# Halo rows of two head pairs copied by DMA from SyncE, a summing matrix zeroed by GpSimd, and a new order of work in a sparse-attention and hardswish kernel

## The chip, the cores and the metric

One core of a Trainium2 chip. The metric is device time of one execution, in microseconds (us). The engines go by the profile's names: PE (TensorE), DVE (VectorE), ACT (ScalarE), POOL (GpSimd), SP (SyncE). Each works through its own list of instructions in order; between engines, semaphores hold an instruction back until what it needs is done.

## The reference

```python
B, H, S, D = 4, 8, 768, 64          # q, k, v
block, window = 32, 16
k_sum = k.reshape(B, H, 24, 32, D).max(axis=3)
v_sum = v.reshape(B, H, 24, 32, D).mean(axis=3)
scores_l = q @ k.T / 8              # masked to |i - j| < 16
scores_s = q @ k_sum.T / 8 + log(32)
a = softmax(concat([scores_l, scores_s]))
x = a @ concat([v, v_sum])          # to [3072, 512]: tokens, heads * D
h = x @ w_in                        # [3072, 2048]
out = (h * clip(h + 3, 0, 6) / 6) @ w_out
```

Each query looks at its neighbours within 16 positions, and at 24 block summaries of the whole sequence. What comes out of all heads goes through two large matrix products with a hardswish between them.

## The kernel before

**Tiles.** Queries go in 12 blocks of 64. For each block the keys and values that it can see are 96 rows: the block itself and 16 on each side. So `vaug[i]` (i is the batch modulo 2) has, for every head and query block, 120 rows on partitions: rows 0 to 31 are the halo, rows 32 to 95 come straight from memory (L424), and rows 96 to 119 are the block means of v. The halo of block t is a copy of rows 64 to 95 of block t - 1, so it can be made out of what is on the chip already. `halo(c, x)` makes it for batch 0, for head pair c (heads 2c and 2c + 1) and half x: x = 0 are blocks 6 to 11, which are worked on first, x = 1 are blocks 0 to 5, the first blocks' half, with block 0 taken from block 11 in a second copy. In the kernel before each is done by DVE or ACT through `copy` (L479). For the other batches the halo is loaded from memory.

**Block sums.** `vsum_first(g)` forms the means of v for pairs 2g and 2g + 1 of batch 0: 24 products (L620) of `ind[:, t]`, a 96 x 32 matrix that says which row belongs to which block, with rows 0 to 95 of `vaug`. Rows 0 to 31 of `ind` must be zero, since halo rows would be counted twice. `ind` is made by POOL (L341 to L344), and its first 32 rows are zeroed by DVE (L347). The sums are copied to `vf` and from there spread over `vaug` rows 96 to 119, for x = 0 early, for x = 1 later.

**Attention.** `k_step` and `q_step` transpose k and q of batch 0 on PE; `scores` forms products of keys and queries (L588), ACT takes exponentials (L597), DVE masks them (L601); `values` multiplies with `vaug` (L709, and L711 with L713 where the means of pairs 2 and 3 come from `vf`). `finish` takes reciprocals (L743), scales (L747), and transposes the result on PE (L781) into `xt`, the input of the MoE half.

**MoE half.** `f1(s, ft)` forms one 128-column piece of h for 384 tokens (L800: four products of 384 columns; for the first three pieces of the first 384 tokens, three groups of four with 128 columns). ACT forms r (L805), DVE the gate (L807). `f2` multiplies with w_out (L820), 16 products for each 128 tokens. Eight stages s of 384 tokens, 512 columns.

**Order.** The kernel records its operations in a plan. `ORDER` is a string with every operation's name in the order in which they are to be planned. A name is a tag and a number: `h031.1` is the second operation of `halo(3, 1)`, `u01.0` the sums of pairs 2 and 3, `v02.0` the first value products of query blocks 4 and 5 in order of work, `K`, `Q`, `V`, `I`, `O` are loads, `F` and `G` the two MoE products. A letter behind a colon chooses the engine where there is a choice (A: ACT, D: DVE, P: POOL, S: SP). `Plan.run` goes through the string, gives each operation a begin from a table of costs, and the operations are then emitted in order of begin. The framework below adds the waits: an instruction waits for the writers, emitted before it, of any rows that it reads, and for the readers of rows that it overwrites.

**Products without use.** Where the plan leaves PE idle within the first 22 us of planned time, `keep` puts products on a constant tile, `idle` (L910), 128 x 512, into a free bank.

**Loads.** All loads are issued by POOL and land by one set of 16 DMA engines. SP issues nothing before the first output is stored at 62.27 us.

Of the kernel before, what the change touches and what calls it, by code (L numbers as in the profile page):

```python
# [15 lines left out]
D = 64  # L16
BLK = 32
# [12 lines left out]
c.0 z1.0:A z3.1:A z0.1:A K00.0 z1.1:D e.3 z0.2 z2.0:D c.8 K01.0 c.1 K02.0 Q000.0 c.2 Q010.0 c.3 k00.0 z0.0:D e.1 z3.0:D c.4  # L30
k01.0 V00.0 V01.0 V02.0 V03.0 c.6 Q01w2.0 Q01w1.0 I0.0 Q01w0.0 k01.2:A k00.1 e.0 k01.1 z2.2 z3.2 z2.1:D k01.4 z1.2 k03.0
k00.3:A k00.2:A k01.3:A q010.0 q010.1:A q000.0 k02.0 q000.1:A k00.4 s000.0 q030.0 s010.0 q020.0 s000.1 s010.1 e.2 k03.1
k02.1 h000.0:D h001.0:D k03.4 c.7 q020.1:D k03.3:A q030.1:A k03.2:A s000.2 s010.2 Q11w0.0 I1.0 I2.0 u00.0 k02.4 h010.0:D
u00.2:A k02.2:A h021.0:D h020.0:D u00.1:D u00.3:D u00.5:D h030.0:D s030.0 s030.1 s020.0 s020.1 s030.2 u01.0 s020.2 I3.0 O0.0
O1.0 K13.0 O2.0 O3.0 K11.0 K10.0 K12.0 u01.2:A u01.1:A v00.0 v01.0 v02.0 v01.1 v00.2 v00.3 v02.2 v02.3 v01.2 v01.3 v00.1
v00.6 v02.1 v00.4 v00.5 v02.4 v02.5 k02.3:A v00.7:A u00.4:A v01.4 v00.8 v00.9:A v01.5:A v02.6 v02.7:A F00.0 F00.10 F00.1
q021.0 q001.0 F00.2 q021.1:A h011.0:D u00.6:D h031.0:D u01.3:D q001.1:D F00.3 F00.11 F00.12 q031.0 F00.4 F00.5 F00.6 F00.7
F00.15 q031.1:A F00.13 F00.8 F00.16 c.5 F00.14 F00.9 F00.17 u01.4:D s031.0 q011.0 s031.1 q011.1:A F01.6 F01.7 s031.2 F01.8
F01.3 F01.4 F01.0 F01.1 F01.5 c.9 F01.2 s001.0 s011.0 s011.1 s011.2 s001.1 s001.2 F02.0 F02.9 F02.1 F02.2 s021.0 F01.9
F02.10 F02.11 F03.0 F02.3 s021.1 F01.10 s021.2 F03.1 F01.11 v03.0 v04.0 F03.2 v03.1 v04.1 v04.2 v03.2 F03.6 F03.9 G02.0  # L40
v03.3 v05.0 F02.4 F03.10 F03.7 F02.5 F03.8 v05.1 v05.2 F02.6 v03.4:A F02.7 v04.3 F03.3 v04.4:D Q11w3.0 V13.0 V12.0 V10.0
V11.0 Q11w4.0 Q11w2.0 Q11w5.0 Q11w1.0 v05.3 G02.1 F03.11 F02.8 v05.4:A F03.4 F03.5 F10.0 F10.1 F10.6 F10.7 F10.2 F10.8 F11.0
F11.1 F11.3 F11.2 F11.4 F11.5 F13.0 F13.1 F13.2 F12.9 F12.6 F12.10 F12.11 F12.7 F12.8 F12.0 F13.6 F12.1 F13.7 F12.2 F13.8
F13.9 F10.3 F13.10 F10.4 F10.5 F13.11 w13.0 G02.2 F10.9 F11.9 F10.10 F10.11 G02.3 F11.6 F12.3 w10.0 w12.0 w11.0 w12.1:D
G02.4:A F12.4 F11.10 w11.1:A G01.0 G01.1 G01.2 G01.3 u1.0 F11.11 G01.4:A F12.5 w11.2 w13.1:A F11.7 w10.1:A u1.1:A u1.6:A
w10.2 w13.2 w10.3:A u1.4:D F11.8 w13.3:D w11.3:D G00.0 G00.1 G00.2 q100.0 q120.0 q110.0 q100.1:A s100.0 s100.3 s100.1 G00.3
q130.0 q120.1:D q110.1:D w12.2 w12.3:D s100.2 u1.8:D u1.2:D s100.4 q130.1:D K23.0 h11.0 K22.0 h10.0 K21.0 Q21.0 K20.0 Q20.0
Q23.0 Q22.0 V22.0 h21.0 V21.0 h20.0 V20.0 V23.0 G00.4:A s110.0 G00.5 F13.3 G12.0 s110.1 s110.3 s120.0 F13.4 s120.3 s120.1
G12.1 G12.2 F13.5 u1.3:D s120.2 s110.2 h1w.0:A s130.0 s130.1 s130.3 G12.3 G12.4:A G12.5 G01.5 s130.2 s110.4 v10.0 s130.4
v10.1 v10.2 v10.5 v10.6 G11.0 G11.1 v12.0 v10.3 u1.9:A u1.7:A u1.5:A v12.1 v12.2 s120.4 w20.0 w20.3 G11.2 v10.4:A v10.7  # L50
v10.8:A v12.3 v12.4:A G11.3 v15.0 v15.1 v15.2 F20.0 G11.4:A F20.1 F20.3 F20.4 F20.6 v13.0 F20.7 F20.2 F20.5 F20.8 v13.5
v13.1 v13.2 F20.9 F22.0 F21.0 w20.2:A F20.10 F22.1 v13.3 F21.1 F20.11 F22.2 F21.2 w20.1 v13.6 F21.6 F22.6 F21.3 v13.4:A
F21.7 F22.7 v15.3 G10.0 v13.7 F21.4 v15.4:A w20.5:A v13.8:A F21.8 F22.8 F21.5 F22.3 F21.9 w20.4:A F22.4 F21.10 F22.9 G10.1
s200.0 w22.0 w21.0 F22.10 w22.2:A s200.3 s200.1 F22.11 F22.5 w23.0 F21.11 G10.2 F23.6 G10.3 F23.0 F23.3 V30.0 V33.0 V31.0
h30.0 h31.0 V32.0 Q33.0 Q31.0 K33.0 Q32.0 K32.0 Q30.0 K31.0 K30.0 F23.7 w21.2:A w21.1 F23.8 G10.4:A F23.1 w21.5:A F23.4 u2.0
u2.1:A u2.2:A F23.9 w21.3 w21.4:D F23.5 w22.1 F23.2 G10.5 G02.5 F23.10 s210.0 F30.9 G20.0 s210.3 u2.4:A u2.5:D w23.1 F23.11
w22.3 G20.1 F30.0 F30.1 F30.10 s210.1 w22.5:A F30.2 w22.4:D F30.11 u2.3:D G20.2 F30.3 G20.3 F30.4 w23.5:A F30.5 w23.3 s210.2
F30.6 G20.4:A F30.7 s210.4 F30.8 s220.0 w23.2:A s220.3 s220.1 w23.4:A F31.3 F33.3 G22.0 u3.0 F31.4 u3.1:A F33.4 s220.4
s220.2 s200.2 F31.5 F32.6 F32.7 s200.4 F33.5 F32.8 s230.0 G22.1 F31.0 G22.2 h2w.0:A s230.1 s230.3 s230.2 s230.4 F32.3 v20.0
F31.9 F31.1 F31.2 v20.1 v20.4 v20.2 v20.5 u3.5:A F31.10 F31.11 F32.0 G22.3 v22.0 v25.0 v20.3 v22.1 v22.2 v22.3 v20.6 F31.6  # L60
u3.3:A G22.4:A F32.4 F31.7 F32.1 F31.8 F32.5 F32.2 w30.1 v22.5:P v22.7:P G21.0 G21.1 G21.2 F33.6 G21.3 F33.7 G11.5 G20.5:S
v22.6:S v22.4:S F33.8 F33.9 F33.0 F32.9 v25.1 w31.1 v25.2 G21.4:A F33.1 G21.5:P G22.5:S F32.10 F32.11 G32.0 G32.1 G32.2
F33.10 F33.11 F33.2 G32.3 h3w.0:A G32.4:A w30.0 w30.3 w31.5:A w30.2:A u3.4:A v23.0 w31.0 G30.0 G30.1 G30.2 F40.0 F42.9
w30.4:A v23.4 v23.5 v23.1 v23.2 v23.3 v25.3 F40.1 F42.10 F40.3 F40.4 F40.2 F42.11 F41.3 F40.5 v23.6 F40.6 F40.9 F41.4 F40.7
F40.10 F41.5 G30.3 G30.4:A F40.8 F40.11 w31.3 F43.9 w30.5:A F43.10 F41.9 F43.6 F41.10 F43.7 F43.11 F41.11 u3.2:A v25.4:S
v25.7:P v25.6:P G32.5:S v25.5:S G30.5:P G31.0 F41.0 F41.6 F43.8 w31.2:D w31.4:D w33.0 F42.6 F41.7 F41.1 F41.8 F42.7 w32.0
F41.2 F42.8 s310.0 G31.1 s310.3 s310.1 F42.3 G31.2 F43.3 F42.0 F42.4 w32.2:A F43.4 F42.1 F42.5 w32.3 F43.0 F43.1 F43.5 F42.2
F43.2 w32.1 w32.5:D s300.0 G31.3 s300.1 w32.4:A s300.3 G31.4:A F50.9 F50.0 F50.6 F50.1 s320.0 w33.1 w33.3 F50.2 G41.0 G41.1
G41.2 F51.9 F50.7 s320.1 s320.2 w33.4:D F50.8 s300.2 w33.5:A w33.2:A s320.3 F50.10 s330.0 s330.1 s330.3 F50.11 s320.4 s310.2
s330.2 G41.3 F51.0 F52.0 G41.4:A v30.0 F52.1 F51.1 s300.4 s330.4 s310.4 v30.4 v30.1 v30.5 F52.2 v30.2 F51.2 v30.3 v30.6  # L70
G42.0 G42.1 G42.2 G42.3 F51.6 v35.0 v32.0 G42.4:A F51.7 F51.10 F52.6 G40.0 G40.1 F52.7 G40.2 v32.1 v32.2 v32.3 v35.1 F51.11
F52.8 F51.8 F50.3 F52.3 F53.3 F50.4 F52.4 F53.4 v35.2 F50.5 G40.3 F51.3 G42.5:S v32.6:P v32.4:P G31.5:S v32.5:S v32.7:S
F52.5 F53.5 F53.6 F51.4 G40.4:A F53.7 G40.5:P F51.5 F53.0 v33.0 F52.9 G50.0 F52.10 F53.1 F53.8 v33.4 v33.5 v33.1 F52.11
F53.2 F53.9 G50.1 G50.2 F53.10 F53.11 G50.3 F60.0 F60.3 F60.1 F60.4 G50.4:D v33.2 F60.2 F60.5 v33.3 v33.6 G52.0 F63.3 F63.4
F63.5 v35.3 G52.1 F61.9 F62.0 F62.1 F61.10 G52.2 G52.3 F61.11 G52.4:D F63.9 F63.10 F62.2 F63.11 F62.9 G51.0 F62.10 F62.11
G50.5:P G41.5:P v35.4:P v35.7:S G52.5:S v35.6:S v35.5:S F61.0 F61.3 F61.4 F61.1 G51.1 F61.5 F61.6 F61.7 F61.8 F60.6 F60.7
F61.2 F60.8 G51.2 F60.9 F60.10 F60.11 F63.0 F63.1 F63.2 G51.3 G51.4:D G51.5:P F63.6 F62.3 F62.4 F62.5 F62.6 G62.0 G62.1
F62.7 F63.7 F62.8 F63.8 G62.2 G62.3 G62.4:A F70.0 F72.9 G60.0 F71.3 F70.1 F71.4 F70.2 F71.5 F72.10 F73.0 G60.1 F73.1 F72.11
F73.2 F70.9 F70.6 F70.7 F70.8 F72.0 G60.2 F72.1 F70.10 F70.11 F72.2 F73.6 F73.7 F73.8 G60.3 G60.4:A F71.9 F72.6 F72.7 F71.10
F71.11 F72.8 G61.0 F70.3 F70.4 F70.5 G61.1 F73.9 F73.10 F73.11 F71.0 F71.1 F71.6 F71.7 F71.8 F71.2 G61.2 F72.3 F72.4 G61.3  # L80
G70.0 G61.4:A F72.5 G62.5:P G61.5:S G71.1 G71.3 F73.3 F73.4 G70.1 G70.2 F73.5 G60.5:S G70.3 G72.0 G72.1 G70.4:D G70.5 G71.5
G72.2 G72.3 G71.0 G71.2 G72.4:A G72.5 G71.9 G71.10:D G71.11 G71.4 G71.6 G71.7:A G71.8
"""

BANKS = ("S", "h", "o")


SLOW = 4.5
TURN = 0.11
LATER = 19.0  # L90
KRAW = 1.6
LAT = {"SP": 0.1, "PE": 0.16, "ACT": 0.08, "DVE": 0.07, "POOL": 0.15}

# [126 lines left out]
def kernel(  # L220
# [83 lines left out]
    def const_ops():  # L304
# [35 lines left out]
        def blocks():  # L340
# [3 lines left out]
            nc.gpsimd.affine_select(out=ind[:], in_=ind[:], compare_op=ALU.is_ge, fill=0.0, base=2 * BLK - 1, channel_multiplier=-1,  # L344
                                    pattern=[[-QB, NQ], [BLK, 32]])
        op("POOL", 1.6, blocks, w=["ind"], prio=-78.5)
        op("DVE", 0.2, lambda: nc.vector.memset(ind[0:BLK], 0.0), w=["ind"], prio=-78)  # L347

        def edges(i):
            t = vaug[i]  # L350
# [606 lines left out]
```

## Time and profile before

| | us |
|---|---|
| time, three runs | 218.79, 220.41, 220.47 |
| median | 220.41 |
| the profiled execution, its own time | 218.78 |
| its span | 217.1 |

| engine | busy us | share of the span | instructions |
|---|---|---|---|
| PE | 207.0 | 95% | 2124 |
| DVE | 165.0 | 76% | 330 |
| ACT | 136.9 | 63% | 271 |
| POOL | 91.0 | 42% | 117 |

| stage (us) | PE busy | DVE busy | ACT busy | POOL busy | DMA share |
|---|---|---|---|---|---|
| 8 to 12 | 3.87 | 3.43 | 2.72 | 3.86 | 1.80 |
| 12 to 16 | 2.75 | 3.27 | 3.22 | 4.00 | 2.44 |
| 16 to 20 | 3.63 | 3.60 | 2.94 | 3.77 | 1.67 |
| 20 to 24 | 3.94 | 3.87 | 3.43 | 2.66 | 1.66 |
| 24 to 28 | 2.96 | 3.87 | 2.72 | 3.11 | 1.24 |
| 28 to 32 | 3.90 | 3.86 | 3.84 | 2.30 | 1.24 |
| 32 to 36 | 3.83 | 3.92 | 2.20 | 1.20 | 1.96 |

The stages are 4 us long, so 4.00 is an engine without a gap. A DMA share over 1 means that packets of more than one transfer were under way in each DMA engine. The span runs from the first to the last recorded event of the program; the time of the execution is 1.7 us longer. In a line of a timeline the first number is the start, the second how long the group of like instructions lasted, then follow engine, line of the kernel, operation, what it writes and reads, how many, and in brackets how long the engine had been idle and what ended that. Ends of products on PE are modelled, so neighbouring groups overlap by 0.1 to 0.2 us.

### The profile page before, as it was taken

To read this page: it belongs to the slowest core of one execution; us is meant where nothing else is said; L and a number is where in the kernel's file an instruction comes from. 1 tells how busy PE (TensorE), PEld (TensorE's weight loads), DVE (VectorE), ACT (ScalarE), POOL (GpSimd) and SP (SyncE) were. 2 spreads that over 40 slices of the span, in tenths; PEclk is the share of its full clock that TensorE was granted. 3 is DMA by queue.
4 is the path that set the end of the run, shared out by engine and by line. 5 is a ranking of instruction groups with operands and counts; after the bars stand their busy time and mean duration, and the time that the engine had idled before them with its cause. 6 is when DMAs were issued, how large, how long until landed. Compare 5 with 4: busy or idle time off the path is not lost.

```text
span 217.1 us, 5338 instructions
## 1 busy us (share of the span) xinstructions
PE 207.0 (95%) x2124; PEld 116.4 (54%) x2151; DVE 165.0 (76%) x330; ACT 136.9 (63%) x271; POOL 91.0 (42%) x117
## 2 busy tenths in 40 slices
PE   6979899999999999999999999999999999999994
PEld 2546656554554565555555555545555555555543
DVE  6889999779798899988898898987865756163310
ACT  8687795664789688998844788963342344345301
POOL 7997944254697856527254073000542401100000
PEclk9999999999999999999999999999999999999999
DMA  5999999999999999999936045000540452100212
GB/s 75 159 155 182 205 207 184 168 138 155 106 125 154 190 148 151 131 204 156 107 35 142 0 77 95 3 0 3 130 91 15 107 90 57 51 0 0 97 51 98
DMA packets 129705, 23.03 MB, mean 106 GB/s; under 512 B 120816, under 2 KB 127152, under 8 KB 129680
## 3 DMA queue, kind: packets, MB, share of 16 engines
q0 software_dynamic: 112656, 17.34, 119.2%
q1 hardware_dynamic: 17024, 5.34, 10.1%
q8 instruction: 17, 0.28, 0.5%
q14 instruction: 8, 0.07, 0.1%
HBM read 29.62 MB, written 6.29 MB: 165 GB/s over the span
## 4 chain that ended last, share of the span: by engine, by line
PE 84%; POOL 4%; DMA 4%; DVE 4%; issue 2%; ACT 2%; POOLq 0%
PE h L800 37%; PE o L820 32%; PE h L820 5%; DMA vaug<-in_v_dram 4%; PE S L709 3%; PE S L588 2%; DVE g L807 2%; POOL vaug L424 1%; PE S L641 1%; POOL first L383 1%; PE S L781 1%; DVE at L601 1%; ACT at L597 1%; POOL first L391 1%; ACT ot L479 0%
## 5 line engine op out<-in xcount | busy, mean ns | idle before, releaser
L800 PE MATMUL h<-x,win 128*128 128x384 bf16 (+1 forms) x536 | 94.3, 319 | 1.3 <-DVE g L807 1.3
L807 DVE SCALAR_TENSOR_TENSOR g<-r,h 128x384 bf16<-128x384 f32 x128 | 67.6, 547 | 29.8 <-ACT r L805 27.5
L805 ACT ACTIVATE r<-h 128x384 f32<-128x384 f32 x128 | 60.6, 492 | 45.9 <-PE h L800 44.4
L820 PE MATMUL o<-wout,g 128*128 128x512 bf16 x312 | 79.0, 379 | 1.6 <-issue 0.5
L800 PEld LDWEIGHTS <-win 128*128 128x128 bf16 x536 | 49.6, 98 | 36.5 <-issue 1.9
L820 PEld LDWEIGHTS <-g 128*128 128x128 bf16 x400 | 38.0, 98 | 36.7
L769 POOL DMA_DIRECT2D x<-y x28 | 17.2, 622 | 40.9 <-issue 22.0
L597 ACT ACTIVATE at<-S 120x768 bf16<-120x768 f32 x32 | 24.7, 813 | 2.4 <-PE S L588 2.4
L424 POOL DMA_DIRECT2D vaug<-in_v_dram x16 | 15.1, 945 | 13.0 <-issue 3.9
L479 ACT COPY ot<-o 128x512 f32<-128x512 f32 x18 | 10.6, 587 | 13.0 <-PE o L820 12.0
L601 DVE TENSOR_TENSOR at<-at,mask 96x768 bf16<-96x768 bf16 x28 | 14.5, 547 | 2.2 <-ACT at L597 1.8
L747 DVE TENSOR_TENSOR xn<-S,rc 128x512 bf16<-128x512 f32 (+1 forms) x24 | 15.7, 661 | 0.5
L413 POOL DMA_DIRECT2D kraw<-in_k_dram x8 | 10.7, 1339 | 8.2 <-issue 4.2
L479 ACT COPY vaug<-vs 24x1536 bf16<-24x1536 bf16 (+1 forms) x10 | 12.1, 1212 | 0.2
L678 DVE TENSOR_REDUCE red<-kaug 128x24 bf16<-128x768 bf16 x12 | 11.1, 941 | 0.1
L820 PE MATMUL h<-wout,g 128*128 128x256 bf16 (+1 forms) x63 | 10.7, 325 | 0.1
L832 POOL DMA_DIRECT2D out_dram<-ot x7 | 4.0, 567 | 14.0 <-DVE ot L479 8.5
L588 PEld LDWEIGHTS <-kaug 64*128 64x128 bf16 x384 | 6.8, 95 | 5.5 <-issue 3.3
L709 PEld LDWEIGHTS <-at 120*64 120x64 bf16 x360 | 6.8, 111 | 4.5 <-issue 3.7
L588 PE MATMUL S<-qT,kaug 64*128 64x64 bf16 x384 | 8.8, 191 | 0.2 <-ACT qT L479 0.2
L910 PE MATMUL o<-idle 128*128 128x512 bf16 x17 | 7.4, 572 | 1.6 <-DVE idle L306 1.5
L709 PE MATMUL S<-vaug,at 120*64 120x65 bf16 x352 | 8.2, 197 | 0.1
(107 smaller groups left out, 181.9 us busy)
## 6 DMA issues: line engine op xcount, KB each, us to landing
vaug<-in_v_dram POOLq DMA_DIRECT2D x22, 192.0 KB, 11.1
out_dram<-ot SPq DMA_DIRECT2D x14, 256.0 KB, 3.1
win<-in_moe_w_in_dram POOLq DMA_DIRECT2D x4, 512.0 KB, 8.5
wout<-in_moe_w_out_dram POOLq DMA_DIRECT2D x4, 512.0 KB, 14.5
kraw<-in_k_dram POOLq DMA_DIRECT2D x8, 192.0 KB, 13.8
out_dram<-ot POOLq DMA_DIRECT2D x5, 256.0 KB, 2.4
first<-in_k_dram POOLq DMA_DIRECT2D x6, 192.0 KB, 6.3
first<-in_q_dram POOLq DMA_DIRECT2D x6, 192.0 KB, 9.0
```

Of the source, the lines that this page charges most:

```text
L424: op("POOL", 0.95, lambda: nc.gpsimd.dma_start(out=o[BLK:WIN, lo:hi, 0:D], in_=rows[:, lo:hi]), w=[("v", b % 2, c)], prio=prio, dma=1.25, ...
L479: {"ACT": nc.scalar.copy, "DVE": nc.vector.tensor_copy, "POOL": nc.gpsimd.tensor_copy}[eng](o, i)
L588: nc.tensor.matmul(X[p, half].slot[:, j, i * QB:(i + 1) * QB], kaug[p][rows, t], qT[rows, p, t * QB:(t + 1) * QB], start=not masked, stop= ...
L597: op("ACT", act(2 * HALF), lambda a=a, x=x: nc.scalar.activation(a, x.slot[0:KEYS, :, 0:HALF], AF.Exp, scale=scl), r=[x], w=[("at", p, hal ...
L601: op("DVE", 0.57, lambda m=m, half=half: nc.vector.tensor_tensor(m, m, mask[:, low(half):low(half) + HQ].unsqueeze(1).to_broadcast([WIN, 2 ...
L709: nc.tensor.matmul(y, a[:, cols], vaug[b % 2][0:KEYS, h, t, 0:D + 1], start=True, stop=True)
L747: nc.vector.tensor_tensor(o, src[..., 0:D], r.unsqueeze(len(r.shape)).to_broadcast(list(o.shape)), op=ALU.mult)
L769: QUEUE[eng].dma_start(out=xt[s].slot[32 * a:32 * a + 32].rearrange("p k (t c j) -> p (k t) c j", t=3, c=4)[:, :, c], in_=ys[s].slot[32 * ...
L800: nc.tensor.matmul(h.slot[:, lo * 128:hi * 128], w_in_sb[:, kt, ft * 128:(ft + 1) * 128], xt[s].slot[:, kt, lo * 128:hi * 128], start=(kt ...
L805: op("ACT", act(HALF), lambda: nc.scalar.activation(r.slot[:], h.slot[:, 0:HALF], AF.Relu, bias=0.5, scale=1.0 / 6.0), r=[h], w=[r], prio= ...
L807: op("DVE", dve(HALF), lambda: nc.vector.scalar_tensor_tensor(gt[s].slot[:, ft], r.slot[:], 1.0, h.slot[:, 0:HALF], op0=ALU.min, op1=ALU.m ...
L820: nc.tensor.matmul(o.slot[:, a:z], gt[s].slot[:, ft, ts * 128:(ts + 1) * 128], w_out_sb[:, ft, a:z], start=(ft == 0), stop=(ft == NFT - 1))
```

## The change

- `halo(c, 1)` for c = 1 and c = 3 (pairs 1 and 3, the first blocks' half of batch 0) is no longer a pair of copies on DVE or ACT. SP issues three DMAs from SBUF to SBUF for each: blocks 1 to 5 of the one head, of the other, and block 0 of both. The value products of that half wait for these too.
- The first 32 rows of `ind` are zeroed by POOL, behind its two selects.
- The table of costs for two kinds of copies is changed, and with it planned begins.
- `keep` has one rule instead of two for how many products to put into a gap, and puts none ahead of block sums. There are 14 instead of 19.
- `ORDER` is a new string throughout. In its head the six operations of SP stand behind the loads of w_in and ahead of the block sums; the two loads of `Q11w0` (q rows of batch 1) stand among the late loads instead of ahead of `I1`.

```diff
 # const_ops
             nc.gpsimd.affine_select(out=ind[:], in_=ind[:], compare_op=ALU.is_ge, fill=0.0, base=2 * BLK - 1, channel_multiplier=-1,
                                     pattern=[[-QB, NQ], [BLK, 32]])
-        op("POOL", 1.6, blocks, w=["ind"], prio=-78.5)
-        op("DVE", 0.2, lambda: nc.vector.memset(ind[0:BLK], 0.0), w=["ind"], prio=-78)
+            nc.gpsimd.memset(ind[0:BLK], 0.0)
+        op("POOL", 1.85, blocks, w=["ind"], prio=-78.5)
 # halo
-        op(EITHER, {"ACT": 0.75 + 0.1 * x, "DVE": 0.42 + 0.1 * x}, go, r=[("v", 0, c), ("vz", 0, c)], w=[("vh", 0, c, x)],
+        if x and c % 2:
+            for h in (2 * c, 2 * c + 1):
+                op("SP", 0.9, lambda h=h: nc.sync.dma_start(out=o[0:BLK, h, a:z, 0:D], in_=o[QB:WIN, h, a - 1:z - 1, 0:D]),
+                   r=[("v", 0, c), ("vz", 0, c), ("vh", 0, c, x)], w=[("vh", 0, c, x, h)], prio=prio, dma=0.37)
+            op("SP", 0.9, lambda: nc.sync.dma_start(out=o[0:BLK, hs, 0, 0:D], in_=o[QB:WIN, hs, NQ - 1, 0:D]),
+               r=[("v", 0, c), ("vz", 0, c), ("vh", 0, c, x)], w=[("vh", 0, c, x, -1)], prio=prio, dma=0.15)
+            return
+        op(EITHER, {"ACT": 0.75 + 0.1 * x, "DVE": 0.45 + 0.35 * x}, go, r=[("v", 0, c), ("vz", 0, c)], w=[("vh", 0, c, x)],
            prio=prio, after=LATER * x)
 # vsum_first
-                op(EITHER, {"ACT": 0.8, "DVE": 0.4}, lambda eng, x=x, c=c: copy(
+                op(EITHER, {"ACT": 0.8, "DVE": 0.4 + 0.15 * x}, lambda eng, x=x, c=c: copy(
 # values
-               + [("vh", b % 2, p, half) for p in ps_] + [("vf", p) if last else ...
+               + [("vh", b % 2, p, half) for p in ps_]
+               + [("vh", 0, p, 1, h) for p in ps_ if p % 2 for h in (2 * p, 2 * p + 1, -1) if b == 0 and half] + [("vf", p) if last else ...
 # the emission, where keep is called
-                n = int((o.begin - end) / 0.43 - 0.4) if end < 1.6 * SLOW else int((o.begin - end) / 0.216 + 0.5)
+                n = int((o.begin - end) / 0.43 - 0.4)
-            if n > 0 and idle_:
+            if n > 0 and idle_ and o.form != "sums":
 # ORDER, around the block sums
-... c.6 Q01w2.0 Q01w1.0 I0.0 Q01w0.0 ... s000.2 s010.2 Q11w0.0 I1.0 I2.0 u00.0 k02.4 h010.0:D
-u00.2:A k02.2:A h021.0:D h020.0:D u00.1:D u00.3:D u00.5:D h030.0:D s030.0 s030.1 s020.0 s020.1 s030.2 u01.0 s020.2 I3.0 O0.0
-... F00.2 q021.1:A h011.0:D u00.6:D h031.0:D u01.3:D q001.1:D F00.3 ...
+... c.6 Q01w2.0 Q01w1.0 I0.0 Q01w0.0 ... k02.2:A I1.0 I2.0 h031.1 h031.0 h011.2 h031.2 h011.0 h011.1
+... s010.2 q030.1:A s000.2 u00.0 u00.2:A u00.5:A u00.1:D u00.3:D s030.0 s030.1 s020.0 s030.2 I3.0 O0.0 O1.0 O3.0 K12.0 O2.0
+K10.0 K11.0 K13.0 h021.0:D v02.0 s020.1 s020.2 h030.0:D v02.2 h020.0:D u01.0 u01.1:A u01.2:A v01.0 v00.0 ...
```

## The prediction, on record before the run

> **What bounds the kernel now.** I read the page first: PE is busy for 207.0 of 217.1 us, so a microsecond counts only where PE waits. The slices put its two weak places at the start and around 25 us. The chain of waits names what ends them:
>
> ```profile
> 6.70 2.75 POOL vaug L424 x3
> 9.46 7.81 DMA vaug<-in_v_dram
> 17.30 0.83 PE h L620 x23
> ...
> 22.13 0.68 PE h L800 x12
> ...
> 24.69 0.36 DVE qT L479
> 25.08 0.56 DVE g L807
> ```
>
> (Columns: start, length, what.) The fourth load of v, that of head pair 3, lands at 9.46 + 7.81 = 17.27. The block sums of pairs 2 and 3 (L620) begin at 17.30; from then PE, DVE and ACT work off one chain (sums, means, values, scaling, transposes), and the first useful product of the MoE half (L800) starts at 21.96 in the timeline, 4.7 us after the landing. Whatever the first 17 us gain is worth nothing unless that load lands earlier. From 22 us PE is almost full: the windows of 4 us show 2.96 busy in 24 to 28 and 3.7 or more after that.
>
> Next the timeline of DVE and of PE behind 17 us:
>
> ```profile
> 18.17 0.35 DVE L479 COPY vaug<-vaug 32x768 bf16<-32x768 bf16 x1 [0.20 <-PE h L620]
> ...
> 21.71 0.59 DVE L479 COPY vaug<-vaug 32x640 bf16<-32x640 bf16 x2
> 22.31 0.70 DVE L479 COPY vaug<-vf 24x768 bf16<-24x768 bf16 x1
> 23.02 1.25 DVE L479 COPY vaug<-vaug 32x640 bf16<-32x640 bf16 x2
> 24.30 0.36 DVE L479 COPY vaug<-vf 24x768 bf16<-24x768 bf16 x1
> ```
>
> ```profile
> 25.69 0.81 PE L800 MATMUL h<-x,win 128*128 128x384 bf16 x4 [1.04 <-DVE g L807]
> ```
>
> The copies at 21.71 and 23.02 are the halos that the change takes off DVE. They stand between the last scaling and the first gate (25.08), and PE waits 1.04 us for that gate.
>
> Last, the time to landing of DMAs on SP's queue: the tile of the output from 60 to 102 us, while POOL's loads keep the DMA engines full, and the DMA issues from 110 us on, when they are mostly quiet:
>
> ```profile
> DMA to landing us min/median/max: 4.3/6.4/7.6
> ```
>
> ```profile
> out_dram<-ot SPq DMA_DIRECT2D x8, 256.0 KB, 2.4
> ...
> x<-y SPq DMA_DIRECT2D x36, 24.0 KB, 2.2
> ...
> out_dram<-ot SPq DMA_DIRECT2D x1, 32.0 KB, 1.6
> ```
>
> From 12 to 36 us the windows have the DMA share between 1.24 and 2.44, so the new copies meet the full case.
>
> **The change, part by part.**
>
> *A new wait ahead of the sums.* This decides. The first of SP's copies (pair 3, head 7, blocks 1 to 5: 160 rows of 128 B, 20 KB) stands in the new program before the sums of pairs 2 and 3. It writes rows 0 to 31 of vaug, and the sums read rows 0 to 95 (rows 0 to 31 against zeros in ind). So the fourth of the 24 products carries a wait for the first DMA of SP's queue; in before the x=1 halos of pairs 1 and 3 came behind the sums. SP cannot issue before v has landed at 17.27, so the wait starts where the chain starts. PE works in order: behind the waiting product stand 20 further products, then all value products, transposes and L800; ACT waits for the sums (means), DVE for the end of the sums (two halo copies) and SP itself, whose second copy overwrites rows that the sums read. Nothing covers it. Price from both sides: 1.6 us, the shortest landing of any SP row, to 6.4, the median with full engines (the 32 KB row there took 6.4 too). I take 4.3, the shortest row under load: this copy is smaller than all of those, but the queue is as full. Landing: 17.27 + 4.3 = 21.6. The other five copies are issued after it and are first read by the values of block 3, which stand at 33.51 in before; hidden.
>
> The Trainium skill ("DMA: Bandwidth & Descriptors", Queues, rings and completion order) says that each DMA engine takes turns between queues, a packet of at most 64 descriptors at a time; by it the copy would pass the backlog and land near the quiet 2.2 us. The loaded SP rows, 4.3 to 7.6 against 1.6 to 2.4, speak for more than that.
>
> *From the sums to the first L800.* The same five reciprocals and five scalings run on DVE. The new order puts two x=0 halo copies (32x768, 0.35 us each at 18.17) behind the sums, where before had one: +0.35. The first product of block 2's early half moves ahead of the sums, but its scaling still stands behind them: 0.
>
> *DVE after that.* 0.59 + 1.25 = 1.84 us of copies leave the stretch before the first gate. PE lost 1.20 there (36 short L800 products take 2.04 and the transposes among them 0.5, of 3.73 from 21.96 to 25.69). Next late is ACT's r (23.40 to 24.89 for the first three), and two copies of means stay, so I book -0.8, bounds -1.2 and -0.4.
>
> *ind on POOL.* The DVE memset (0.22) goes, and with it the PE wait of 1.25 at 14.44; but that lies ahead of 17.27: 0. If no wait for v followed it would be worth up to 1.25. POOL gains a memset of 32x384; the nearest row is 96x384, 0.44. It delays the issues of qwide and of the first win chunk, whose landing at 21.06 had 0.9 us to the first L800 and now has more: 0. The two q rows of batch 1 move from behind that chunk to behind K of batch 1: the later win chunks come about 1.4 us earlier (0.62 + 0.83 of issue), and the SP copies put some 0.6 us of packets in (768 of 128 B; a v load of 1536 takes 1.25 between landings). Both hidden: before had v of batch 1 landed at 53.30 for sums at 54.78, and PE now comes later.
>
> *Fewer products on idle.* 14 instead of 19. Behind 17.27, four fall away (0.2 to 0.3 us each), all in gaps where PE waited for DVE or ACT: 0. If they had delayed the chain, -0.3.
>
> *Rest of the order.* The useful products are the same, and so is the count of entries from full products into those on part of the rows, 30 behind the first L800, some 0.1 us each (L820 takes 0.96 instead of 0.86 ahead of scores). Around 58 to 68 us PE loses about 1 us to ACT's exponentials; there the new order puts one L820 group (0.86) ahead of the scores instead of among them, and moves the wrap copy (0.62) from ACT to DVE: +0.25, bounds -0.6 and +0.86. The tail has the same last copy and store: 0.
>
> Sum: 4.3 + 0.35 - 0.8 + 0.25 = +4.1 us. Against the profiled execution, 218.78 (span 217.1 and 1.7 around it), that is 222.9. The other two runs of before took 220.41 and 220.47, so the median lies 1.6 above it; as a median I forecast 220.41 + 4.1 = 224.5.
>
> **Rivals.**
> - The copy lands as if the engines were quiet (2.2, the x<-y row; the rows under load speak against it). Then 2.2 + 0.35 - 0.8 + 0.25 = +2.0: 220.8 to 222.4. By the rule on turns this would be the likely case.
> - The wait also drops PE's clock. While PE waits from about 17.5 to 21.6 it has nothing to do, and at the start of this execution 7 products of 512 columns on idle take 3.17 us, later 16 of L820 take 3.62: half speed, until about 9.7 us. If PE falls back and needs as much as half of that stretch again, some 4 us of its work take twice as long: +2 to +4 on top, 226.5 to 228.5. Against it: no row shows a fall after a pause, and the page grants full clock throughout, at the slow start too. The Trainium skill ("TensorE: Matmul & The Clock Gate", Part 1: The HAM clock gate) halves the clock after some 3.4 us without work; no pause here is long enough to test it.
> - Not slower: the copy lands in 1.6, the DVE relief brings 1.2, the exponentials 0.6: 1.6 + 0.35 - 1.2 - 0.6 = +0.15, 218.9 to 220.6. It decides where the landing stays under about 2 us, and only if every gain is at its best end. Faster needs, beyond this, the idle products to have delayed the chain (-0.3) and more that no row shows.
> - The change does not do what it says: SP's copies might not shorten DVE's list at all if others fill the gap. Then the -0.8 goes: 225.3, inside the range.
>
> **How the numbers follow.** The wait at 3.5 to 6.5 us with the clock kept: 0.55, 223.5 to 226.5; with the clock lost: 0.20, 226.5 to 229.5; quiet landing: 0.17; not slower: 0.08, of it 0.03 faster. Within 1% (2.2 us, about what can be told from no change) fall the 0.05 and some 0.06 of the quiet case. So faster 0.03, same 0.11, slower 0.86. The range goes from the quiet case on the profiled run, 221.0, to the middle of the clock case, 229.0.
>
> **What would show it.** In the profile after: a wait of PE at the sums of pairs 2 and 3 on an SP copy of vaug, 2 to 6 us long, and the chain passing through that DMA; first L800 at about 26 instead of 21.96; its wait for the first gate under 0.4; from there to the end the same length within 1 us. L820 or L800 at double spacing right after the wait would be the clock. It is wrong if the sums start right after v's landing, or if the copy's landing is under 2 us.

## The result, and the profile after

The changed kernel is slower: four runs took 227.41, 227.6, 227.75 and 229.1 us (median 227.68), beside 219.74 for the kernel before in the same comparison. The ratio is 1.040 with a 95% interval of 1.036 to 1.043. The profiled execution took 227.6 us, its span is 225.9 (before 217.1): +8.8. A ratio leaves out executions more than 1.5% above the fastest of their kernel, so where single executions differ much (a2, e1, d4 below) the median of all lies above what the ratio says.

The chain of waits of the changed kernel, from 17 us on (start, length, what):

```profile
17.00 0.17 DVE vaug L486
17.17 5.96 DMA vaug<-vaug
23.13 0.04 issue
23.18 1.34 PE o L627 x21
```

The load of v is no longer the last link: its successor is SP's copy, 5.96 us from issue to landing. PE's timeline shows the same wait from the other side, and more (L627 are the block sums, the old L620; L808 is the old L800):

```profile
10.06 0.36 PE L545 MATMUL o<-ident,first 96*64 96x96 bf16 x8 [1.73 <-DMA first<-in_q_dram]
...
18.62 0.28 PE L627 MATMUL o<-vaug,ind 96*32 96x128 bf16 x3
23.18 1.33 PE L627 MATMUL o<-vaug,ind 96*32 96x128 bf16 x21 [4.28 <-DMA vaug<-vaug]
...
29.71 2.99 PE L808 MATMUL h<-x,win 128*128 128x128 bf16 x32
```

Three products of the sums ran, the fourth waited 4.28 us. And the 21 left took 1.33 us: in before 23 took 0.83. That is the clock. These are windows of PE (stretch, length, PE busy and products, granted clock as a share of full speed, DMA share, GB/s), cut where the clock changes:

```profile
7.99:11.40 3.41, 1.63 (x54) 1.00 1.73 174
11.40:14.81 3.41, 3.00 (x48) 0.50 2.43 159
14.81:18.22 3.41, 3.41 (x48) 0.50 2.04 164
18.22:21.64 3.42, 0.68 (x23) 1.00 1.52 190
21.64:25.05 3.41, 1.87 (x37) 0.50 1.30 210
25.05:28.46 3.41, 2.45 (x52) 0.50 1.26 207
28.46:31.88 3.42, 3.42 (x37) 0.50 1.42 214
31.88:35.29 3.41, 3.41 (x48) 1.00 1.25 207
```

Half clock twice, 6.8 us long after a pause of 1.73 us (PE waits for q at 8.3 to 10.06), and 10.2 us long after the pause at the sums. In the profile before, every window of 4 us from 8 to 36 us has 1.00.

The new copies among the DMA issues from 10 to 35 us (tile, queue, how many, KB each, median us to landing), and DVE behind the last scaling:

```profile
vaug<-vaug SPq DMA_DIRECT2D x4, 20.0 KB, 5.9
vaug<-vaug SPq DMA_DIRECT2D x2, 8.0 KB, 5.4
```

```profile
29.69 0.63 DVE L486 COPY vaug<-vf 24x768 bf16<-24x768 bf16 x2
32.19 1.18 DVE L815 SCALAR_TENSOR_TENSOR g<-r,h 128x384 bf16<-128x384 f32 x2 [1.86 <-ACT r L813]
```

DVE is free early now and waits 1.86 us for r, and PE's wait of 1.04 us for the first gate is gone. (The 0.21 us that PE still waits for a gate in after, at 39.59, stands in before too, at 32.12.)

Where the 8.8 us lie, read off marks of the timelines. The last column is run c1 below: the same order without the wait and with ten more products on idle, profiled at a mean clock of 0.998:

| stretch | before | after | difference | without the wait (c1) |
|---|---|---|---|---|
| start to the sums of pairs 2 and 3 (in after: to where they go on) | 17.30 | 23.18 | +5.88 | 18.25 |
| to the first L800 / L808 | 4.66 | 6.53 | +1.87 | 5.40 |
| to the values of block 3 (33.51 in before) | 11.55 | 11.27 | -0.28 | 10.27 |
| to the end | 183.59 | 184.92 | +1.33 | 184.88 |
| span | 217.1 | 225.9 | +8.8 | 218.8 |

The marks that no other view here shows, two of before, one of after and one of c1:

```profile
21.96 0.84 PE L800 MATMUL h<-x,win 128*128 128x128 bf16 x12
33.51 0.70 PE L709 MATMUL S<-vaug,at 120*64 120x65 bf16 x32
...
40.98 0.99 PE L716 MATMUL S<-vaug,at 120*64 120x65 bf16 x32
...
33.92 0.99 PE L716 MATMUL S<-vaug,at 120*64 120x65 bf16 x32
```

After minus c1: 4.93 of wait at the sums, and 1.13 + 1.00 = 2.1 us behind it, which I put down to the half clock (the ten products differ too). c1 minus before, that is the rest of the change (order, relief of DVE, zeroing by POOL): +0.95, +0.74, -1.28, +1.29 = +1.7.

### The profile page after: what moved, and what is told of

It is laid out like the page before. It is cut to its first block, busy times and chain, and to the rows that moved or that the text cites. A ratio compares the mean times of both kernels' runs of the same rounds, so it can differ in the third digit from the quotient of the medians.

```text
span 225.9 us, 5349 instructions
## 1 busy us (share of the span) xinstructions
PE 209.7 (93%) x2123; PEld 119.3 (53%) x2146; DVE 164.4 (73%) x322; ACT 137.7 (61%) x274; POOL 91.6 (41%) x119
## 4 chain that ended last, share of the span: by engine, by line
PE 86%; DMA 5%; ACT 3%; issue 2%; DVE 2%; POOL 1%; ACTq 0%; POOLq 0%
PE h L808 37%; PE o L828 31%; PE h L828 5%; PE S L595 3%; PE S L716 3%; DMA vaug<-vaug 3%; DMA first<-in_q_dram 3%; ACT at L604 2%; PE o L627 1%; PE S L648 1%; PE S L789 1%; POOL first L383 1%; DVE vaug L486 1%; ACT ot L486 1%; PE S L586 1%
## 5 line engine op out<-in xcount | busy, mean ns | idle before, releaser
L808 PE MATMUL h<-x,win 128*128 128x384 bf16 (+1 forms) x536 | 94.2, 322 | 0.3 <-DVE g L815 0.2
L828 PE MATMUL o<-wout,g 128*128 128x512 bf16 x313 | 78.1, 379 | 1.6 <-issue 0.5
L808 PEld LDWEIGHTS <-win 128*128 128x128 bf16 x536 | 50.6, 100 | 34.8 <-issue 0.5
L424 POOL DMA_DIRECT2D vaug<-in_v_dram x16 | 15.1, 945 | 9.6 <-issue 5.8
L486 ACT COPY ot<-o 128x512 f32<-128x512 f32 x19 | 11.1, 586 | 12.7 <-PE o L828 12.7
L840 POOL DMA_DIRECT2D out_dram<-ot x9 | 5.0, 559 | 23.2 <-ACT ot L486 23.2
L486 ACT COPY vaug<-vs 24x1536 bf16<-24x1536 bf16 (+1 forms) x10 | 12.1, 1212 | 0.2
L453 POOL DMA_DIRECT2D vaug<-in_v_dram x6 | 5.4, 911 | 13.0 <-ACT r L813 11.9
L828 PE MATMUL h<-wout,g 128*128 128x512 bf16 (+1 forms) x64 | 10.6, 326 | 0.0
L595 PE MATMUL S<-qT,kaug 64*128 64x64 bf16 x384 | 9.4, 195 | 0.7 <-ACT qT L486 0.6
L486 DVE COPY vaug<-vaug 32x768 bf16<-32x768 bf16 (+3 forms) x9 | 4.0, 463 | 7.5 <-PE o L627 7.4
```

The lines of the kernel that those rows point to most:

```text
L424: op("POOL", 0.95, lambda: nc.gpsimd.dma_start(out=o[BLK:WIN, lo:hi, 0:D], in_=rows[:, lo:hi]), w=[("v", b % 2, c)], prio=prio, dma=1.25, ...
L486: {"ACT": nc.scalar.copy, "DVE": nc.vector.tensor_copy, "POOL": nc.gpsimd.tensor_copy}[eng](o, i)
L595: nc.tensor.matmul(X[p, half].slot[:, j, i * QB:(i + 1) * QB], kaug[p][rows, t], qT[rows, p, t * QB:(t + 1) * QB], start=not masked, stop= ...
L808: nc.tensor.matmul(h.slot[:, lo * 128:hi * 128], w_in_sb[:, kt, ft * 128:(ft + 1) * 128], xt[s].slot[:, kt, lo * 128:hi * 128], start=(kt ...
L828: nc.tensor.matmul(o.slot[:, a:z], gt[s].slot[:, ft, ts * 128:(ts + 1) * 128], w_out_sb[:, ft, a:z], start=(ft == 0), stop=(ft == NFT - 1))
```

## The experiments

Theory A: the wait for SP's first copy, and the half clock that follows the pause, make nearly all of the loss.

**a1: the copy behind the sums.**

```diff
     order = plan.run()
+    moved = next(o for o in order if o.key == "h031.1")
+    order.remove(moved)
+    order.insert([o.key for o in order].index("u01.0") + 1, moved)
```

> The changed kernel with one instruction moved: SP's copy for head 7 of pair 3 is issued behind the block sums of pairs 2 and 3 instead of ahead of them. Theory A (the wait for that copy, and the half clock that follows the pause, are nearly all of the loss): PE no longer waits 4.28 us at these sums; they start at 18.6, where PE arrives at them in the changed kernel because of its first stretch at half clock (11.3 to 17.9 us), the first L808 comes at 23.2 to 24.0 instead of 29.7, and the time is 5.5 to 7 us under the changed kernel and 1 to 2.5 over the kernel before (ratio 1.004 to 1.012). Theory B (the new order behind 22 us is what costs): the time falls by less than 3 us, ratio above 1.02. Theory C (the relief of DVE pays once the wait is gone): ratio under 1.0.

222.57 us, ratio 1.014 (1.011 to 1.017). One instruction moved takes 5.1 us off. The sums start at 18.23 with nothing but a 0.20 us wait for DVE ahead of them, the first L808 comes at 24.04. But 3 us remain, more than I had expected, and the windows of a1 say where the next part is:

```profile
13.62:17.03 3.41, 1.85 (x40) 1.00 2.34 157
17.03:20.44 3.41, 2.01 (x64) 1.00 1.52 185
20.44:23.85 3.41, 3.41 (x59) 0.50 1.34 206
23.85:27.28 3.43, 3.43 (x35) 0.50 1.42 213
```

The clock falls here too, and stays at half for 6.8 us from 20.44. No wait in the window ahead of that fall is longer than 0.94 us; the wait of 2.07 us that ends at 15.18, in the window before, was followed by full clock.

**b1: the wait alone, in the old kernel.** SP copies the rows of head 7 ahead of the sums; DVE still copies them later.

```diff
+        if o.key == "u01.0":
+            todo.append(lambda: nc.sync.dma_start(out=vaug[0][0:BLK, 7, 1:HQ, 0:D],
+                                                  in_=vaug[0][QB:WIN, 7, 0:HQ - 1, 0:D]))
         todo.append(o.fn)
```

> The kernel before with one SP copy added ahead of the block sums of pairs 2 and 3 (the same 160 rows of head 7; DVE's own copy of the same rows stays and writes the same data again later). Nothing else of the change is in it. Theory A (wait of about 5.9 us, then half clock from about 3 us into the pause until about 8 us after its end): +7 to +8.5, 226.8 to 228.2, granted clock 0.5 from about 21 to 31 us. Rival, clock lost only together with the earlier pause of the changed kernel: +5.5 to +6.2, full clock throughout. Rival, landing as I took it before (4.3): +4.3 to +5, and no fall of the clock or a short one.

227.49 us, ratio 1.036 (1.032 to 1.040): one DMA of 20 KB brings nearly the whole loss of the change (1.040).

```profile
19.11 0.28 PE L620 MATMUL h<-vaug,ind 96*32 96x128 bf16 x3
23.10 1.33 PE L620 MATMUL h<-vaug,ind 96*32 96x128 bf16 x21 [3.70 <-DMA vaug<-vaug]
```

That the totals are so close is in part chance: the stretch to the sums grows by 5.80 us here and the one to the first L800 by 2.73 (7.39 against 4.66), while the rest of the change, 1.7 us in c1, is absent. The copy took 5.28 us (17.78 to 23.06), and the clock was at half from 22.3 to 32.6 us. It also fell from 12.1 to 15.5 us in this execution, where K landed late and PE had waited 2.26 us for it.

**a2: PE kept busy in the wait.**

```diff
+            if o.key == "u01.0":
+                todo.append(lambda s=o.alloc[0].slot: keep(18, s))
```

> The changed kernel with 18 products of 512 columns on idle data (0.216 us each at full clock, 3.9 us in all) put on PE right ahead of the block sums of pairs 2 and 3, into the bank that the sums then overwrite. The wait for SP's copy stays, PE is busy during most of it. Theory A: the landing stays at 23.1, the granted clock stays at 1.0 behind it, the first L808 comes 1.2 to 1.8 us earlier and the short L808 products after it take 57 ns instead of 87, so 2 to 2.8 us under the changed kernel (ratio to the kernel before 1.024 to 1.029). Rival, the half clock behind the wait is hidden by DVE's and ACT's chain: less than 0.7 under the changed kernel.

The four executions took 224.69, 225.71, 227.97 and 228.75 us at mean clocks of 0.992, 0.985, 0.977 and 0.977; ratio 1.031 (1.025 to 1.037). The idle products did not hold the clock in the profiled execution: it was at half from 16.4 to 19.8 us already, behind a wait of 2.00 us ahead of the first sums, and it fell again at 26.6 us, behind waits of 1.15 us (the rest of the landing) and 1.17 us (a copy of DVE). The fastest execution is 3.0 under the changed kernel's median.

**a3: behind the sums, and PE kept busy from 8.3 to 10 us.** a1, and:

```diff
+            if o.key == "q010.0":
+                n += 7
             if n > 0 and idle_ and o.form != "sums":
```

> The changed kernel with the SP copy behind the sums (as in a1) and 7 more products on idle data ahead of the first transposes of q, so that PE is busy from 8.3 to 10.06 us where it waited for the load of q. Theory A: the granted clock stays at 1.0 throughout; the sums start at 17.3, right behind the landing of v, the first L808 comes at 22.0 to 22.6, and the time equals the kernel before within 1 us (ratio 0.996 to 1.005), 0.8 to 1.5 under a1. Theory C (relief of DVE pays in full): ratio 0.994 to 0.997. Theory B (new order costs): ratio above 1.01. Rival on the clock: if the fall at 11.3 us in the changed kernel had another cause than the pause ahead of it, this run shows the same fall and the time of a1.

222.19 us, ratio 1.014 (1.010 to 1.018): no gain over a1. What the early pause costs stays open, since it was down to 0.20 us in a1's profiled execution already, and the products on idle last until 11.82 us here, so that the first products on q start 1.5 us later than in a1 (10.35). The clock falls all the same, later than in a1:

```profile
17.21:20.63 3.42, 2.63 (x75) 1.00 1.44 182
20.63:24.04 3.41, 2.79 (x63) 1.00 1.31 207
24.04:27.45 3.41, 3.41 (x36) 0.50 1.43 213
27.45:30.86 3.41, 3.41 (x40) 1.00 1.30 209
```

In the 3.41 us ahead of that fall PE was busy for 2.79, mostly with small products (65 or 128 columns, some on 24 rows). So a long pause is not needed. That made theory D: with fewer products on idle, PE's work between 13 and 24 us is too thin for the clock.

**c1: a1 with the old rule for idle products (24 of them instead of 14).**

```diff
-                n = int((o.begin - end) / 0.43 - 0.4)
+                n = int((o.begin - end) / 0.43 - 0.4) if end < 1.6 * SLOW else int((o.begin - end) / 0.216 + 0.5)
-            if n > 0 and idle_ and o.form != "sums":
+            if n > 0 and idle_:
```

> The changed kernel with the SP copy behind the sums (as in a1) and the old rule for products on idle data: 10 more of them between 11 and 24 us (one ahead of the second transposes of q, 5 ahead of the sums of pairs 0 and 1, one before the first values, 3 among the transposes of the first values). Theory D (what is left of the loss in a1 and a3, +3 us, is the clock, which falls because fewer products on idle leave PE's work from 13 to 24 us too thin): mean granted clock 0.99 or more, ratio 1.000 to 1.006, 1.8 to 3 us under a1. Rival E (the clock falls for another reason, or the rest of the new order costs the 3 us): ratio 1.011 to 1.018 as in a1, with the same clock.

221.6 us, ratio 1.013 (1.009 to 1.018). Executions at clocks of 0.998 and 0.992 took 220.5 to 221.7, those at 0.985 and 0.977 took 223.1 and 223.7; a1 had 0.977 to 0.985 throughout. The idle products help the clock, but the ratio that theory D wanted did not come: 1.7 us stand in the profiled execution at nearly full clock, as the table above has them. They begin here:

```profile
18.25 0.85 PE L627 MATMUL o<-vaug,ind 96*32 96x128 bf16 x24 [0.21 <-DVE vaug L486]
...
20.41 0.32 PE L718 MATMUL S<-vaug,at 96*64 96x65 bf16 x8 [0.94 <-DVE vaug L486]
...
23.65 1.95 PE L808 MATMUL h<-x,win 128*128 128x128 bf16 x32
```

The last v landed at 16.93, but the new order has PE busy with scores, values of block 2 and an idle product until 18.04; and the two halo copies behind the sums hold the next values for 0.94 us.

**c2: the rule for idle products alone, in the old kernel** (the two lines of c1 the other way round; 13 products instead of 19).

> The kernel before with the new rule for products on idle data alone: 13 instead of 19, those missing stood at 11.34, 18.57, 20.87 and 21.52 us of its profile, one ahead of the sums of pairs 2 and 3 and one more beside that of 21.52. No SP copy, the old order. Theory D: the granted clock falls to 0.5 for some 3 to 7 us somewhere between 18 and 30 us in most executions, mean clock 0.975 to 0.99, ratio 1.006 to 1.014. Prediction on record (fewer products cost nothing, or gain 0.3 us): ratio 0.998 to 1.001, clock 1.0.

219.88 us against 218.87, ratio 1.0032 (0.9999 to 1.0066): too close to call as a ratio. The clocks are clearer: 7 of 12 executions had 0.984 or less, against 1 of 23 of the kernel before beside them. Those seven took 219.6 to 221.4 us, the five others 218.7 to 219.4. So the rule makes a longer fall likely, and it costs 1 to 2 us; it does not come each time.

**e1: the wait left in, the old rule, and 20 idle products ahead of the sums.**

```diff
+            if o.key == "u01.0":
+                todo.append(lambda s=o.alloc[0].slot: keep(20, s))
```

> The changed kernel, with the wait for the SP copy left where it is, the old rule for products on idle data (10 more) and 20 further ones (4.3 us at full clock) right ahead of the sums of pairs 2 and 3, so that PE has work before and during the wait. Theory A (wait and clock are two costs): the copy still lands 5 to 6 us after its issue and the sums go on at 23 to 24.5 us, the mean granted clock is 0.985 or more, and the time is that of the version without wait at full clock (220.5) plus the wait's 4 to 5 us: 224.3 to 225.6, ratio 1.023 to 1.030, against 1.040 for the changed kernel. Rival (the clock is only a record and costs nothing, the whole loss is the wait): ratio 1.036 to 1.043.

Six executions: 224.33 us at a clock of 0.999, 226.76 and 226.97 at 0.992, 228.18 to 229.49 at 0.985; ratio 1.032 (1.027 to 1.037), above what I expected, since the clock fell in five of six, in the profiled one at 26.7 us behind waits of 2.27 (the copy took 6.50 us here) and 1.38. The one execution at full clock is 5.4 us above the kernel before (218.97), but that holds the rest of the change too. Against c1 near full clock, 220.51 beside a kernel before of 218.87, the wait alone is 3.8 us, less than the 4.93 of the table; it is one execution without a profile. The five others took 2.4 to 5.2 us longer than it. How much of that is clock and how much landing is not shown, since only one of them was profiled.

**c3: SP's copies where DVE's stood, in the old kernel** (behind the sums), with the zeroing by POOL.

```diff
         def go(eng):
+            if x and c % 2:
+                for h in (2 * c, 2 * c + 1):
+                    nc.sync.dma_start(out=o[0:BLK, h, a:z, 0:D], in_=o[QB:WIN, h, a - 1:z - 1, 0:D])
+                nc.sync.dma_start(out=o[0:BLK, hs, 0, 0:D], in_=o[QB:WIN, hs, NQ - 1, 0:D])
+                return
```

> The kernel before with the six SP copies in place of DVE's x=1 halo copies of pairs 1 and 3, issued where those stood (behind the sums, the values and the transposes), and the zeroing of the summing matrix by GpSimd; old order, old rule for idle products. Relief of DVE as I priced it: PE's wait of 1.04 us for the first gate goes, -0.8 (bounds -1.2 and -0.4): ratio 0.994 to 0.998, clock 1.0. Rival, the relief brings nothing because ACT's r is next late, or the copies disturb the loads: ratio 0.999 to 1.004.

219.84 us, ratio 1.0055 (1.003 to 1.008): slower, against both of my forecasts. The relief is there (the first scores behind the first MoE products stand at 25.40 instead of 26.43), but two thirds of it are lost to gates that wait for DVE before batch 1 plays a part: the values of block 3 start at 33.15 instead of 33.51. The rest is gone by 55 us, where the sums of batch 1 stand 0.53 later than in before. The chain of waits of c3:

```profile
19.62 11.25 DMA win<-in_moe_w_in_dram
...
31.38 18.08 DMA kraw<-in_k_dram
```

It is the last load of K of batch 1, landing at 49.46; in before it landed at 47.92 and was in no chain. Theory F: PE cannot be earlier than batch 1's loads.

**d1: c3 without the zeroing by POOL, and with the q rows of batch 1 loaded later**.

```diff
-... s000.2 s010.2 Q11w0.0 I1.0 I2.0 ...
+... s000.2 s010.2 I1.0 I2.0 ...
-V11.0 Q11w4.0
+V11.0 Q11w0.0 Q11w4.0
```

> The kernel before with the six SP copies in place of DVE's halo copies (as in c3), without the zeroing by GpSimd, and with the load of the first q rows of batch 1 moved behind the loads of its v, so that the loads of K of batch 1 are issued earlier. Theory F (in c3 the relief, -1.0 us at 25 us, was given back because the last load of K of batch 1 landed at 49.5 us, later than before): the lead of 1 us at 25 us lasts to the sums of batch 1 (54.78 in before), ratio 0.994 to 0.998. Rival (it is given back elsewhere, by gates that wait for DVE at 28 to 32 us, or the relief ends at another bound): ratio 0.999 to 1.005, and the sums of batch 1 stand at 54.5 to 55.4.

219.07 us, ratio 1.000 (0.997 to 1.002). PE leads by 1.20 us from 26 to 38 us; the last K lands at 48.39, and at the sums of batch 1 the lead is 0.71, behind the loads of q 0.28.

**d3: d1 with K of batch 1 ahead of the last two chunks of w_out.**

```diff
-O1.0 K13.0 O2.0 O3.0 K11.0 K10.0 K12.0
+O1.0 K13.0 K11.0 K10.0 K12.0 O2.0 O3.0
```

> As d1 (six SP copies in place of DVE's halo copies in the kernel before, first q rows of batch 1 loaded later), and the loads of K of batch 1 are issued ahead of the last two chunks of w_out instead of behind them. Theory F (in d1 the lead of 1.2 us that PE has from 25 to 48 us ends at the last load of K of batch 1, which lands at 48.4): K then lands at 44 to 46.5, and the lead of at least 0.9 us is still there at the sums of batch 1 (54.78 in before) and at the end, ratio 0.993 to 0.997. Rival (the last w_out chunk, or the loads of q and v behind it, are late instead): ratio 0.998 to 1.006.

219.47 us, ratio 1.000 (0.998 to 1.003). K landed at 44.15, as planned, and the next load took its place:

```profile
53.16 6.25 DMA qraw<-in_q_dram
...
59.45 0.49 PE S L569 x10
```

PE waits for the last q of batch 1. This execution began late (its last v landed at 17.66, and PE reached the sums of pairs 2 and 3 at 18.07 instead of 16.96); it had made good 0.9 us by 55 us and lost it again by 60.

**d4: the moves of loads of d3 alone** (the two diffs of `ORDER` above, without the SP copies).

> The kernel before with the two moves of loads of d3 alone, without SP copies. In before PE does not wait for K of batch 1 (landing 47.9 us), so theory F expects no change: ratio 0.998 to 1.002, and the difference between d3 and this run is the relief of DVE (-0.9 to -1.2 us). Rival (the order of the loads is worth something by itself): ratio under 0.997.

220.33 us, ratio 1.005 (1.002 to 1.008), where I expected no change. Its profiled execution shows two losses. The clock was at half from 15.5 to 18.9 us, behind a wait of 1.77 us, so PE reached the sums at 17.75 instead of 16.96 although the last v landed early (16.98); and PE waited 1.31 us for the first gate instead of 1.04. Whether the other executions lost in the same way is open: 7 of 12 have a mean clock of 0.992 or less, against 6 of 23 of the kernel before beside them and 6 of 12 of d3. d3 is 0.6 us faster than d4 if the three longest of d4 (222.9 to 223.1) are left out of its median (219.47, 220.04), and 1.1 by the ratios. That would fit the relief, but with d4's own loss unexplained it is not shown. No version beat the kernel before.

## Why the prediction was right, and where it was not

The direction, the place and the mechanism of the wait were right: the new wait at the sums decides, b1 gives it alone, a1 takes it away. The range held. The likeliest time, 224.5, was 3.2 us too low, and luck made that look better than it is: the sum of +4.1 stood on a median of 220.41, and the kernel before took 219.74 in the comparison, so the change cost 7.9 us. On the profiled executions, +8.8, the sum lacked 4.7 us: 2.1 of half clock, 1.6 of landing, 1.1 in the rest of the order and 0.4 between the sums and the first L808, less 0.5 of relief that was better than booked.

- **The landing.** Priced 4.3, measured 5.96: the term was mis-sized. I took the shortest row of SP under load because the copy was small, but size hardly mattered: the copies of 8 KB took 5.4 us beside 5.9 for 20 KB. In the four kernels that wait at the sums (changed, b1, a2, e1) it took 5.96, 5.28, 7.07 and 6.50: the median under load, 6.4, was the better row, and the upper bound of 6.4 too low. The whole stretch grew by 5.88 us where I had 4.3, and not more, although the new order reaches the sums later (c1: 18.25), since the wait hides that.
- **The quiet rival**: it did not come. No packet of SP's queue moved from the issue at 17.17 until 21 us, while POOL's queue moved 1,707; then the 176 packets of SP's queue moved in the 2.2 us up to the landing. In the quiet part of before, the first packets of an SP copy issued at 125.87 moved 1.2 us later. The Trainium skill ("DMA: Bandwidth & Descriptors", Queues, rings and completion order) says that each DMA engine takes turns between queues, a packet at a time. The trace agrees from the first packet on, with 98 of SP's packets beside 114 of POOL's from 22.0 to 22.6 us. The landing near 2 us that I read from that rule did not follow; what holds the copy for the 3.8 us ahead of its first packet is open.
- **The clock rival** got 0.20, and it came true. "No row shows a fall after a pause" was true of the page and a weak argument: the kernel before has 19 products on idle in its gaps, so its rows cannot show what happens without them. It costs 1.13 from the sums to the first L808 and 1.00 behind it, the +2 that I had as the lower end. This is the step that failed: the likeliest case put at nothing a term that came in all four executions (mean clocks of 0.955 to 0.970). The Trainium skill ("TensorE: Matmul & The Clock Gate", Part 1: The HAM clock gate) says that the gate watches a free-running window of about 3.4 us and halves the clock after an idle one. The grid agrees: 3.4, 6.8 and 10.2 us at half in these runs. The condition does not, if idle means without work: the clock fell behind windows in which PE was busy for 2.0 of 3.41 us (a1) and 2.79 (a3).
- **From the sums to the first L808, +0.35.** c1 shows +0.74 at full clock: two halo copies were right in number, but the second took 0.61 us there, and in after 0.97 instead of 0.35, so the values waited for 0.94 to 0.96.
- **DVE relief, -0.8 (bounds -1.2, -0.4).** Mis-sized: -1.28 in c1 and -1.20 in d1, at and just beyond my better end. But c3, d1 and d3 show that in the old order it is given back, in c3 first to later gates, and then in all three because batch 1's loads become the last to come. In after PE is 7 us later than the loads, so it keeps the relief; it just pays more elsewhere.
- **Zeroing on POOL, 0.** The wait for `ind` at 14.44 goes, hidden as said (in a1, PE waits 2.07 us for ACT at the same sums instead). In c3 the loads behind it were issued some 0.5 us later, which may be part of why K was late; it was not tried alone.
- **Fewer idle products, 0 or -0.3.** Wrong in kind: their price is the clock. c2 shows it as a chance, 7 of 12 against 1 of 23, worth 1 to 2 us when it happens.
- **Rest of the order, +0.25 (up to +0.86).** Measured +1.33. The last 57 us make 0.8 of it (from the values at 159.97 to the end 57.13 in before, 57.95 and 57.99 in c1 and after); but executions in before's order show 57.06 (c2) and 57.96 (b1) there, so this much is not shown to be the order. The exponentials at 60 to 70 us are in what is left, +0.5.

Signs named beforehand: the wait on SP's copy, 2 to 6 us (4.28), the chain through it, the gate's wait under 0.4 (gone), and double spacing for the clock, all came. "First L800 at about 26" did not (29.71), and "the same length within 1 us" from there to the end was just missed (196.2 against 195.1).

## What to carry to other kernels

A copy that is moved to a DMA is emitted at a place and writes a range of rows: see who reads any of those rows next in program order, even rows that it multiplies by zero, and issue the DMA behind them. Price a wait of PE as landing plus what the clock loses, some 2 us in the changed kernel, and count products on idle as part of the clock, not as filling. Relief on an engine is worth what the next bound leaves of it: look up when the loads for the next stage land before booking it.

## What the runs showed of the hardware

The clock changes on a grid of 3.41 us within one execution (falls at 11.40 and 21.64 are three steps apart) and differs from execution to execution of one kernel. Busy time alone does not decide: a window with 1.85 us of PE work kept it (a1, 13.62 to 17.03), one with 2.79 us of small products lost it (a3). Nor does it alone decide when full clock comes back: in c2 that took three windows with PE busy for 3.26, 3.42 and 3.41 us, in a3 one with 3.41. What counts instead was not settled.

A small copy on DVE sometimes takes longer while POOL issues a DMA. Timeline of all engines in after, from 24 us:

```profile
24.43 1.41 POOL L413 DMA_DIRECT2D kraw<-in_k_dram  x1 [0.41 <-DMA win<-in_moe_w_in_dram]
...
24.54 0.35 DVE L486 COPY vaug<-vaug 32x768 bf16<-32x768 bf16 x1 [6.33 <-PE o L627]
...
25.02 0.97 DVE L486 COPY vaug<-vaug 32x768 bf16<-32x768 bf16 x1
```

The same copy took 0.35 us when it began 0.1 us behind the start of the issue, and 0.97 when it began in its middle; it then ended 0.15 us after the issue. The Trainium skill ("SBUF — State Buffer", Who interferes with whom) describes a pair of ports that DVE, in some modes, and GpSimd lock against each other for a whole instruction. The second copy would fit that, the first would not, and in before the copy at 18.17 took 0.35 while POOL issued from 17.55 to 19.80. No run here takes the issue away, so the cause is open.
